# Windowed attention with a gated feed-forward block: the sigmoid gate made from tanh and exp instead of a reciprocal

## The chip, the cores and the metric

One Trainium2 chip, of which the kernel uses one core. The metric is the time of one launch on the device in microseconds (us). The core has five engines that run side by side and wait for one another by semaphores: TensorE (PE in the profile, with its weight loads shown apart as PEld), VectorE (DVE), ScalarE (ACT), GpSimd (POOL) and SyncE (SP), which issues the DMAs. Each engine works through its own instructions in order.

## The reference

The inputs are q, k, v of shape (8, 8, 576, 64) and the weights of a gated block, all float32. First comes attention in which each row sees itself and the 63 rows before it, then a block that mixes each row with the row before it:

```python
scores = scale * np.matmul(q, k.transpose(0, 1, 3, 2))
mask = (rel >= 0) & (rel < 64)                 # rel = row - column
attn = softmax(np.where(mask, scores, -1e9))   # with 1e-9 added to the sum
x = np.matmul(attn, v)                         # put together to (8, 576, 512)

x_prev = x shifted by one row
xk = mu_k * x + (1.0 - mu_k) * x_prev
xr = mu_r * x + (1.0 - mu_r) * x_prev
k = np.maximum(xk @ w_k, 0.0)                  # 512 -> 1024
v = k * k @ w_v                                # 1024 -> 512
r = 1.0 / (1.0 + np.exp(-(xr @ w_r)))          # the gate, 512 -> 512
return r * v
```

## The kernel before, in words

The rows of all batches lie one behind the other, 4608 in all, and are cut into blocks of 64. The gated block is computed in eleven *units* of 4, 5 and then nine times 7 blocks, so that a matmul of the units 2 to 10 has 448 columns. A unit has three phases on TensorE. The k phase makes `xk @ w_k` in 8 column tiles, the r phase `xr @ w_r` in 4, and the v phase `k*k @ w_v` in 4. Every float32 operand is split into a high and a low part, and a product takes three matmuls for each 128 rows of the contraction. So a k or r tile takes 12 matmuls and a v tile 24, and a unit 240. Unit 0 runs r, k, v, the others k, r, v.

The order is written out by hand: every engine keeps the order in which the Python code issues its work. Six matmuls of the gated block are one *step* of a clock, and a unit has 40 steps. Work is issued at a step (`at_step`) or so many steps later (`later(n, fn)`). Between the matmuls of the units stands the attention of later blocks, in *groups* of 8 blocks at the steps in the table `BEGIN`. A group goes like this:

- `scores`: 32 matmuls (`s<-k,q`).
- `soften`, for each half of the group: VectorE adds the mask and takes the row maximum, ScalarE takes exp and the row sum. Both write `pr`.
- `norm`: VectorE makes the reciprocal of the row sum (`rs`), GpSimd multiplies `pr` by it.
- `flip`: TensorE transposes `pr` (`t<-ident,pr`) into the one PSUM buffer `t`; `keep`: ScalarE copies that to SBUF (`COPY pt<-t`). The second half's flip stands two steps, 12 matmuls, behind the first's, and needs both its own normalized `pr` and the buffer `t` emptied by the first half's copy.
- `values`: matmuls with v (`x<-pt,v`), one group later, and a copy to `xT`.

The next unit's inputs are made by `mix`, in the steps 25 to 31 (xk) and 33 to 39 (xr) of a unit: VectorE makes `d` with two instructions for each piece, ScalarE rounds it to the high part (`CAST xk<-d`), GpSimd subtracts to get the low part (`xk<-d,xk`).

The change touches the end of an r tile (`r_units`) and the end of a v tile (`gated`). In the r phase, one step behind the last matmul of a tile ScalarE runs `power` on the tile's PSUM bank, and two steps behind it VectorE runs `share`. The result waits in one of four buffers `r` until the v tile of the same number is done. Then `gated` multiplies them on VectorE and SyncE stores the result. The pool tag `tmp` has five buffers that rotate among the weights' decoding (`wt`, at the start only), the mixed `d` and the k phase's `kf`.

At the start, to about 130 us, the weights arrive as float64 and are decoded to float32 by ScalarE and VectorE (`wt`, `wp`, `ws`), beside unit 0.

Of the kernel before, what the change touches and what calls it, by code (L numbers as in the profile page):

```python
# [9 lines left out]
F32 = mybir.dt.float32  # L10
F32R = mybir.dt.float32r
U32 = mybir.dt.uint32
AF = mybir.ActivationFunctionType
ALU = mybir.AluOpType
PSUM = bass.MemoryType.PSUM

P = 128
# [7 lines left out]
TU = max(UNITS) * W  # L25
# [3 lines left out]
FAR = 3.0e38  # L29
SCALE = 1.0 / D**0.5  # L30
R_BUFS = 4
WC = 512
XB = 9
TB = 5
# [15 lines left out]
def attn_rwkv_kernel(ctx, tc, qT, kT, v2, mu_k, mu_r, w_k, w_v, w_r, out):  # L50
# [5 lines left out]
    tmp = ctx.enter_context(tc.tile_pool(name="tmp", bufs=2))  # L56
# [16 lines left out]
    pe, dve, sca, pool = (Engine(e) for e in (nc.tensor, nc.vector, nc.scalar, nc.gpsimd))  # L73
# [3 lines left out]
    def later(steps, fn, *args):  # L77
        due.setdefault(now + steps, []).append((fn, args))
# [14 lines left out]
    for first in (None, 0, 1):  # L93
        masks[first] = const.tile([P, P], F32, name=f"mask{first}")
        nc.gpsimd.memset(masks[first], 0.0)
        for j in range(2):
            m = masks[first][j * W:(j + 1) * W]
# [218 lines left out]
    def parts(u):  # L316

        t, end = sum(UNITS[:u]) * W, sum(UNITS[:u + 1]) * W
        found = []
        while t < end:  # L320
            n = min(end, (t // S + 1) * S) - t
            found.append((t // S, t % S, n))
            t += n
        return found
# [22 lines left out]
    def weight(w, a, c, m):  # L347

        o = m * P
        return w[c, o // WC][:, a, o % WC:o % WC + P]  # L350

    def product(ps, w, col, x, n):

        for c in range(n):
            for a, e in ((0, 0), (0, 1), (1, 0)):
                pe.matmul(ps, weight(w, a, c, col), x(c, e), start=(c == 0 and a == e),
                          stop=(c == n - 1 and a == 1))
                yield

    def r_units(xr, gate, n):  # L360

        for m in range(NC):
            ps = ps_m.tile([P, 512], F32, name="m", tag="m")[:, :n]
            yield from product(ps, wr_s, m, lambda c, e: xr[:, e, c, :n], NC)

            def power(ps=ps):
                r = tmp.tile([P, TU], F32, name="r", bufs=R_BUFS)[:, :n]
                sca.activation(r, ps, AF.Exp, scale=-1.0)
                gate.append(r)

            def share(m=m):
                dve.tensor_scalar(gate[m], gate[m], FAR, 1.0, op0=ALU.min, op1=ALU.add)
                dve.reciprocal(gate[m], gate[m])

            later(1, power)
            later(2, share)

    def k_units(xk, k2, n):
# [21 lines left out]
                later(1 + i, fn)  # L400

    def gated(u, m, ps, o):
        dve.tensor_mul(o, ps, o)
        c0 = 0
        for b, t0, nt in parts(u):
            nc.sync.dma_start(out[b, m * P:(m + 1) * P, t0:t0 + nt], o[:, c0:c0 + nt])
            c0 += nt

    def v_units(u, k2, gate, n):
        for m in range(NC):  # L410
            ps = ps_m.tile([P, 512], F32, name="m", tag="m")[:, :n]
            yield from product(ps, wv_s, m, lambda c, e: k2[c][:, e], NF)
            later(1, gated, u, m, ps, gate[m])

    def v_first(u, k2, gate, n):


        acc = [ps_m.tile([P, 2, n], F32, name="mv", tag="m") for _ in range(NC // 2)]
        for f in range(NF):
            for m in range(NC):  # L420
                for a, e in ((0, 0), (0, 1), (1, 0)):
                    pe.matmul(acc[m // 2][:, m % 2], weight(wv_s, a, f, m), k2[f][:, e],
                              start=(f == 0 and a == e and m % 2 == 0),
                              stop=(f == NF - 1 and a == 1 and m % 2 == 1))
                    yield
        for m in range(NC):
            later(1, gated, u, m, acc[m // 2][:, m % 2], gate[m])
# [88 lines left out]
    for u, nb in enumerate(UNITS):  # L516
        n = nb * W
        xr, xk = mixed
        gate, k2 = [], []
# [12 lines left out]
        def work():  # L532
            if u == 0:
                yield from r_units(xr, gate, n)
                yield from k_units(xk, k2, n)
                yield from v_first(u, k2, gate, n)
            else:
                yield from k_units(xk, k2, n)
                yield from r_units(xr, gate, n)
                yield from v_units(u, k2, gate, n)  # L540
# [40 lines left out]
```

## Time and profile before

| | |
|---|---|
| median of 3 runs | 762.38 us (760.97 to 764.76) |
| the profiled execution | 762.73 us |
| its span, first to last instruction | 760.5 us |
| mean granted TensorE clock | 0.941 of full speed |
| busy: PE / DVE / ACT / POOL | 668.5 / 514.2 / 351.2 / 332.7 us |

The span leaves out 2.2 us of the profiled execution's own time. A line of the profile's groups names the engine, the operation, the tile written and those read (buffer numbers left out), and its shape; behind it stand the count, the busy time, the mean of one in ns, and the idle time of the engine before it with what ended that. Line L71 is the helper through which all compute instructions are issued, so tiles and not lines tell the instructions apart. `m` is a PSUM bank that a product is summed in, `ks` the split k*k, `ws` split weights. A timeline row gives the start, the duration, and in brackets how long the engine had stood idle and what it waited for.

### The profile page before, as it was taken

The page shows a single profiled execution, that of the slowest core. Times are in us where ns is not written, and L with a number is a line of the kernel's source. Part 1 is how long each engine was busy: PE and PEld are TensorE (multiplying, and loading weights), DVE is VectorE, ACT ScalarE, POOL GpSimd, SP SyncE. Part 2 cuts the span into 40 slices and gives each one's busy share as a digit, 9 for nine tenths or more (in the row PEclk, how much of TensorE's full clock was granted, in tenths as well). Part 3 has the DMA queues.
Part 4 walks back from the last instruction along what each step waited for, and adds up shares of the span by engine and source line. Part 5 has one row for each costly group of instructions (what it writes and reads, how often), then busy time and mean ns, then how long its engine had stood idle before and what let it go on. Part 6 is the DMA issues. An engine that isn't in the chain of part 4 may idle for free.

```text
span 760.5 us, 14297 instructions
## 1 busy us (share of the span) xinstructions
PE 668.5 (88%) x5232; PEld 593.7 (78%) x5232; DVE 514.2 (68%) x1328; ACT 351.2 (46%) x1067; POOL 332.7 (44%) x503
## 2 busy tenths in 40 slices
PE   3556657898998999899979989998998997999998
PEld 2446556887887888698869989887886996999997
DVE  4789797358439926954883595497388549739562
ACT  4556645544653455356434535534654562242330
POOL 4544645524651653445254355435425642432610
PEclk9958877999999899999999999999999999999999
DMA  7961201222310122132111112122221200100101
GB/s 243 302 245 63 84 32 60 87 72 92 109 60 28 69 72 77 59 127 84 60 38 60 38 60 85 59 72 97 64 84 56 84 1 7 43 0 13 37 1 49
DMA packets 33766, 56.50 MB, mean 74 GB/s; under 512 B 5024, under 2 KB 16800, under 8 KB 33696
## 3 DMA queue, kind: packets, MB, share of 16 engines
q1 hardware_dynamic: 33696, 55.59, 21.9%
q8 instruction: 41, 0.67, 0.4%
q14 instruction: 29, 0.24, 0.1%
HBM read 46.14 MB, written 9.44 MB: 73 GB/s over the span
## 4 chain that ended last, share of the span: by engine, by line
PE 52%; DVE 23%; issue 9%; ACT 7%; POOL 4%; DMA 3%; SPq 1%; POOLq 0%; ACTq 0%
PE m L71 41%; DVE r L71 9%; DVE d L71 6%; ACT pr L71 4%; PE s L71 4%; PE x L71 3%; PE t L71 3%; POOL pr L71 3%; DVE wp L71 2%; DVE pr L71 2%; DVE wt L71 2%; DMA w<-w_k 2%; DVE rs L71 2%; POOL kf L71 1%; PE mv L71 1%
## 5 line engine op out<-in xcount | busy, mean ns | idle before, releaser
L71 POOL TENSOR_SCALAR pr<-pr,rs 128x128 f32<-128x128 f32 x288 | 123.3, 447 | 232.3 <-DVE nmax L71 157.8
L71 PE MATMUL m<-xk,ws 128*128 128x448 f32 (+2 forms) x1056 | 215.8, 358 | 5.6 <-POOL ws L71 3.0
L71 PE MATMUL m<-ks,ws 128*128 128x448 f32 (+1 forms) x960 | 208.7, 375 | 0.0
L71 PEld LDWEIGHTS m<-xk,ws 128*128 128x128 f32 x1056 | 188.4, 191 | 18.5 <-POOL ws L71 3.2
L71 PEld LDWEIGHTS m<-ks,ws 128*128 128x128 f32 x960 | 184.0, 198 | 14.1
L71 ACT ACTIVATE pr<-pr,nmax 128x128 f32<-128x128 f32 x288 | 113.0, 395 | 79.9 <-DVE nmax L71 79.9
L71 DVE TENSOR_TENSOR ks<-kf,ks 128x448 fp32r<-128x448 f32 (+2 forms) x88 | 56.4, 640 | 125.3 <-ACT ks L71 125.3
L71 DVE RECIPROCAL r<-r 128x448 f32<-128x448 f32 (+2 forms) x44 | 121.9, 2771 | 1.5
L71 PE MATMUL t<-ident,pr 128*128 128x128 f32 x288 | 60.1, 315 | 65.7 <-ACT pt L71 42.6
L71 PE MATMUL m<-xr,ws 128*128 128x448 f32 (+2 forms) x528 | 112.6, 364 | 3.9 <-ACT xr L71 2.2
L71 POOL TENSOR_TENSOR kf<-kf 128x448 f32<-128x448 f32 (+2 forms) x88 | 78.0, 886 | 77.4 <-ACT kf L71 77.3
L71 PEld LDWEIGHTS t<-ident,pr 128*128 128x128 f32 x288 | 38.6, 153 | 86.3 <-POOL pr L71 44.4
L71 PEld LDWEIGHTS m<-xr,ws 128*128 128x128 f32 x528 | 95.5, 195 | 11.4 <-ACT xr L71 2.6
L71 ACT CAST ks<-kf 128x448 fp32r<-128x448 f32 (+2 forms) x88 | 47.5, 540 | 68.0 <-POOL kf L71 67.9
L71 DVE TENSOR_TENSOR d<-xT 128x256 f32<-128x256 f32 (+6 forms) x136 | 77.5, 570 | 0.1
L71 DVE CUSTOM_DVE_ANT_0 pr<-s,maskNone 128x128 f32<-128x128 f32 x224 | 55.0, 282 | 27.5 <-PE s L71 27.5
L71 POOL TENSOR_TENSOR xr<-d,xr 128x448 fp32r<-128x448 f32 (+2 forms) x44 | 51.5, 1176 | 35.3 <-ACT xr L71 35.0
L71 POOL TENSOR_TENSOR xk<-d,xk 128x448 fp32r<-128x448 f32 (+2 forms) x44 | 52.6, 1206 | 28.3 <-ACT xk L71 28.3
L71 ACT COPY xT<-x 128x256 f32<-128x256 f32 (+7 forms) x68 | 23.3, 391 | 70.6 <-PE x L71 70.6
L71 ACT ACTIVATION_READ_ACCUMULATOR pr<-pr,nmax 128x1 f32 x288 | 54.6, 190 | 0.0
L71 ACT COPY pt<-t 128x512 f32<-128x512 f32 (+1 forms) x74 | 42.2, 570 | 26.2 <-PE t L71 26.1
L71 PE MATMUL s<-k,q 64*64 64x128 f32 x1152 | 46.5, 305 | 6.6 <-DMA q<-qT 4.5
(42 smaller groups left out, 589.0 us busy)
## 6 DMA issues: line engine op xcount, KB each, us to landing
v<-v SPq DMA_DIRECT2D x56, 256.0 KB, 3.9
k<-kT SPq DMA_DIRECT2D x28, 288.0 KB, 2.8
q<-qT SPq DMA_DIRECT2D x28, 288.0 KB, 3.7
w<-w_k SPq DMA_DIRECT2D x8, 512.0 KB, 7.2
w<-w_v SPq DMA_DIRECT2D x8, 512.0 KB, 10.2
outT<-r SPq DMA_DIRECT2D x12, 224.0 KB, 1.9
w<-w_r SPq DMA_DIRECT2D x4, 512.0 KB, 4.9
outT<-r SPq DMA_DIRECT2D x12, 160.0 KB, 1.8
```

The costliest lines, as they stand in the source:

```text
L71: return lambda *args, **kw: tc.keep_in_program_order(op(*args, **kw))
```

## The change

The gate is computed in another way. For z = `xr @ w_r`, before: ScalarE makes exp(-z), VectorE clips it and adds 1, and takes the reciprocal. Now: ScalarE makes `th` = tanh(z/2) and `r` = exp(z). VectorE takes min(exp(z), 1), clears the sign bit of `th` by a bitwise and on its words read as integers, and makes (|th| + 1) * min(exp(z), 1), which is twice the gate. The factor 0.5 enters in `gated`, in the same instruction as the product with the v tile. `th` takes a buffer of the tag `tmp`.

```diff
         for m in range(NC):
             ps = ps_m.tile([P, 512], F32, name="m", tag="m")[:, :n]
             yield from product(ps, wr_s, m, lambda c, e: xr[:, e, c, :n], NC)
-
-            def power(ps=ps):
-                r = tmp.tile([P, TU], F32, name="r", bufs=R_BUFS)[:, :n]
-                sca.activation(r, ps, AF.Exp, scale=-1.0)
+            state = []
+
+            def powers(ps=ps, state=state):
+                state += [tmp.tile([P, TU], F32, name="th", tag="tmp", bufs=TB)[:, :n],
+                          tmp.tile([P, TU], F32, name="r", bufs=R_BUFS)[:, :n]]
+                sca.activation(state[0], ps, AF.Tanh, scale=0.5)
+                sca.activation(state[1], ps, AF.Exp)
+
+            def share(state=state):
+                th, r = state
+                dve.tensor_scalar(r, r, 1.0, None, op0=ALU.min)
+                dve.tensor_scalar(th.bitcast(U32), th.bitcast(U32), 0x7FFFFFFF, None, op0=ALU.bitwise_and)
+                dve.scalar_tensor_tensor(r, th, 1.0, r, op0=ALU.add, op1=ALU.mult)
                 gate.append(r)
 
-            def share(m=m):
-                dve.tensor_scalar(gate[m], gate[m], FAR, 1.0, op0=ALU.min, op1=ALU.add)
-                dve.reciprocal(gate[m], gate[m])
-
-            later(1, power)
+            later(1, powers)
             later(2, share)
...
     def gated(u, m, ps, o):
-        dve.tensor_mul(o, ps, o)
+        dve.scalar_tensor_tensor(o, ps, 0.5, o, op0=ALU.mult, op1=ALU.mult)
```

No instruction moves past another: on PE, POOL and SP the order is the same, and on VectorE and ScalarE the new ones stand where the old ones stood. Two places matter later. The first is VectorE in the r phase of unit 2, the first of 448 columns; `pr` and `nmax` belong to the group whose scores stand between the r tiles. Before:

```order
L71 TENSOR_SCALAR r<-r 128x448
L71 RECIPROCAL r<-r 128x448
L71 TENSOR_SCALAR r<-r 128x448
L71 RECIPROCAL r<-r 128x448
L71 TENSOR_SCALAR r<-r 128x448
L71 RECIPROCAL r<-r 128x448
L71 ISA pr,nmax<-s,mask_101 128x128
L71 ISA nmax 128x1
```

And now, in the same place:

```order
L71 TENSOR_SCALAR r<-r 128x448
L71 TENSOR_SCALAR th<-th 128x448
L71 SCALAR_TENSOR_TENSOR r<-th,r 128x448
L71 TENSOR_SCALAR r<-r 128x448
L71 TENSOR_SCALAR th<-th 128x448
L71 SCALAR_TENSOR_TENSOR r<-th,r 128x448
L71 TENSOR_SCALAR r<-r 128x448
L71 TENSOR_SCALAR th<-th 128x448
L71 SCALAR_TENSOR_TENSOR r<-th,r 128x448
L71 ISA pr,nmax<-s,mask_101 128x128
L71 ISA nmax 128x1
```

Two instructions for a tile have become three, and the next group's softmax still stands behind three r tiles.

The second place is ScalarE at the same time, from the end of the k phase to the fourth r tile; `pt` are the copies of the transposes, `xT` the attention's output. Before:

```order
L71 CAST ks<-kf 128x448
L71 ACTIVATE r<-m 128x448
L71 COPY pt<-t 128x512
L71 ACTIVATE r<-m 128x448
L71 COPY pt<-t 128x512
L71 ACTIVATE r<-m 128x448
L71 COPY xT<-x 128x512
```

And now:

```order
L71 CAST ks<-kf 128x448
L71 ACTIVATE th<-m 128x448
L71 ACTIVATE r<-m 128x448
L71 COPY pt<-t 128x512
L71 ACTIVATE th<-m 128x448
L71 ACTIVATE r<-m 128x448
L71 COPY pt<-t 128x512
L71 ACTIVATE th<-m 128x448
L71 ACTIVATE r<-m 128x448
L71 COPY xT<-x 128x512
```

Each copy of a transposed half now stands behind one activation more. The program has one row `ACT_TABLE_LOAD` on ScalarE, at its start, both before and now.

## The prediction

> **What bounds the kernel now.** I read the busy shares first, then the slices, then who waited for whom on TensorE, and last the time rows of the places where it waits.
>
> ```profile
> PE 668.5 (88%) x5232; PEld 593.7 (78%) x5232; DVE 514.2 (68%) x1328; ACT 351.2 (46%) x1067; POOL 332.7 (44%) x503
> PE   3556657898998999899979989998998997999998
> DVE  4789797358439926954883595497388549739562
> PE t L71 <- ACT pt L71: 42.6, 15, 5.3
> ```
>
> TensorE bounds the kernel, apart from the first 130 us. But it has regular dents, and VectorE is full (9) just where TensorE dents. Its longest waits stand in front of the transposes `t`. The dents lie in the r phases of units 1 to 8. Of their stretches, here are unit 2's, ten us within it, unit 8's, and the time after that:
>
> ```profile
> core 0: us, PE busy (x) PEld busy (x) DVE busy (x) ACT busy (x) POOL busy (x), PEclk, DMA share, GB/s
> 220.00:256.00 36.00, 32.95 (x250) 27.48 (x250) 30.68 (x71) 14.95 (x46) 13.65 (x22) 0.91 0.14 47
> 230.00:240.00 10.00, 10.00 (x103) 8.77 (x102) 9.88 (x16) 2.90 (x12) 0.00 (x0) 1.00 0.17 54
> 620.00:652.00 32.00, 26.97 (x177) 23.22 (x176) 26.61 (x45) 10.98 (x31) 10.70 (x14) 0.89 0.02 8
> 650.00:760.00 110.00, 106.85 (x546) 99.57 (x544) 64.88 (x76) 29.57 (x54) 32.63 (x29) 1.00 0.07 24
> ```
>
> TensorE idles 3.1 us in unit 2's row and 5.0 in unit 8's, and its mean clock is 0.91 and 0.89. In the last row no attention is left, and it runs without a dent. Unit 2 shows the mechanism:
>
> ```profile
> 227.69 0.54 ACT L71 ACTIVATE r<-m 128x448 f32<-128x448 f32 x1
> 228.13 0.58 ACT L71 COPY pt<-t 128x512 f32<-128x512 f32 x1
> 228.85 0.63 PE L71 MATMUL t<-ident,pr 128*128 128x128 f32 x4
> 231.87 1.10 PE L71 MATMUL s<-k,q 64*64 64x128 f32 x32
> 235.25 2.95 DVE L71 RECIPROCAL r<-r 128x448 f32<-128x448 f32 x1
> 238.39 0.41 ACT L71 ACTIVATE pr<-pr,nmax 128x128 f32<-128x128 f32 x1 [3.70 <-DVE nmax L71]
> 241.52 1.48 PE L71 MATMUL t<-ident,pr 128*128 128x128 f32 x4
> 241.72 2.95 DVE L71 RECIPROCAL r<-r 128x448 f32<-128x448 f32 x1
> 246.64 0.56 ACT L71 CAST xk<-d 128x448 fp32r<-128x448 f32 x1 [0.91 <-DVE d L71]
> 247.07 2.27 POOL L71 TENSOR_SCALAR pr<-pr,rs 128x128 f32<-128x128 f32 x4 [3.35 <-DVE rs L71]
> 247.84 1.25 PE L71 MATMUL t<-ident,pr 128*128 128x128 f32 x3 [2.44 <-ACT pt L71]
> 249.40 0.47 PE L71 MATMUL t<-ident,pr 128*128 128x128 f32 x1 [0.31 <-POOL pr L71]
> 254.26 1.10 PE L71 MATMUL s<-k,q 64*64 64x128 f32 x32
> ```
>
> The scores are done at 233, but VectorE is in the third of three reciprocals until 238.2, and the group's softmax stands behind them. The fourth reciprocal (241.7 to 244.7) holds up its second half. Where the wait is called `ACT pt`, the copy stands on ScalarE behind a `CAST xk` that itself waits for VectorE's `d`: here too VectorE is late.
>
> **What the dents cost.** From the first of these two flips to the next scores there are 8 transposes and 24 matmuls. Undisturbed, the same takes 5.84 us:
>
> ```profile
> 409.61 0.60 PE L71 MATMUL t<-ident,pr 128*128 128x128 f32 x4
> 415.45 1.10 PE L71 MATMUL s<-k,q 64*64 64x128 f32 x32
> 570.87 1.51 PE L71 MATMUL t<-ident,pr 128*128 128x128 f32 x4 [0.87 <-POOL pr L71]
> 582.05 1.10 PE L71 MATMUL s<-k,q 64*64 64x128 f32 x32
> 249.87 4.46 PE m L71 x12
> 413.11 2.41 PE m L71 x12
> ```
>
> In unit 2 it took 254.26 - 241.52 = 12.74, an excess of 6.9 us. That holds the idle time, transposes that go at GpSimd's pace, and 12 matmuls at a lower clock afterwards (4.46 for 2.41, in the last two rows, which are of the chain). Unit 7, in the middle rows, has 582.05 - 570.00 - 5.84 = 6.2, with its first flip wanted 0.87 before it starts. The same difference in units 3 to 6 gives 6.5, 6.9, 2.3 and 5.0. Unit 8, with half the transposes and no scores behind, has some 7.5, and unit 1, whose matmuls have 320 columns, 6.0. Together 47 us (6.0+6.9+6.5+6.9+2.3+5.0+6.2+7.5 = 47.3).
>
> On the clock, the Trainium skill's page "TensorE: Matmul & The Clock Gate" (section "HAM oscillation — how this bites in real kernels") says that idle gaps above about 3.4 us let the clock fall. By that rule unit 2's wait of 2.44 us would have cost no speed, and only units with longer gaps would lose any; some 8 us of the loss (the slow matmuls of the five units with shorter gaps, 1 to 2 us each) would then have another cause and might stay, for a time near 723. The trace differs: the clock mean is 0.91 over unit 2's row and the 12 matmuls took 4.46 us, so I count the slow matmuls with the gap that they follow.
>
> **The change part by part.**
>
> ```profile
> L71 DVE RECIPROCAL r<-r 128x448 f32<-128x448 f32 x36 | 106.3, 2953 | 1.2
> L71 DVE TENSOR_SCALAR r<-r 128x448 f32<-128x448 f32 x36 | 13.5, 376 | 1.5 <-ACT r L71 1.5
> L71 DVE TENSOR_TENSOR ks<-kf,ks 128x448 fp32r<-128x448 f32 x72 | 45.2, 627 | 114.2 <-ACT ks L71 114.2
> L71 DVE SCALAR_TENSOR_TENSOR d<-d,mur,xT 128x448 f32<-128x448 f32 x12 | 11.3, 941 | 0.4
> L71 DVE TENSOR_SCALAR wp<-wt 128x512 uint32<-128x512 uint32 x20 | 13.9, 695 | 0.7
> L71 ACT ACTIVATE r<-m 128x448 f32<-128x448 f32 x36 | 19.5, 541 | 14.6 <-PE m L71 14.6
> L71 ACT ACT_TABLE_LOAD x1 | 1.3, 1283 | 0.7 <-PEq L573 0.7
> ```
>
> VectorE, a tile of 448: out goes the reciprocal, 2.95 us. The clip stays one TENSOR_SCALAR of 0.38. The bitwise and is not in the trace; it lies between the float form, 0.38, and the integer form into PSUM, 0.69. I take 0.38, since it reads and writes SBUF as that does. The new (|th|+1)*min lies between two-tensor rows, 0.63 and 0.94; I take 0.64, as it has no operand by partition. So 3.33 becomes 1.40, a saving of 1.9 us (1.3 at the dear ends), and 7.7 for a unit's four (5.3). That is 70 us of VectorE's busy time on 36 tiles, of which only what lay in the dents counts.
>
> Does that clear a dent? Unit 2's first half-softmax, at 238.1, stood behind three tiles. They now end near 234: scores at 233, third exp at about 232, 1.4 behind it. The four behind it make the second half 6 to 7.5 us earlier. TensorE wants that half at 241.52 + 0.35 + 2.5 = 244.4 and had finished its transposes at 249.9 for 244.8, so 5 are needed: the dent goes, with 1 to 2 us to spare. The late link next is ScalarE's `COPY pt` behind `CAST xk`, which moves forward with `d`. Units 4 and 8 have the least to spare; in unit 8 I leave 0.5. With the dear ends, 5.3 just covers 5, and some 1 us would remain in each unit. In unit 1 the first pair of flips has a wait that isn't this one:
>
> ```profile
> 164.88 0.43 ACT L71 ACTIVATE r<-m 128x320 f32<-128x320 f32 x1
> 165.21 0.58 ACT L71 COPY pt<-t 128x512 f32<-128x512 f32 x1
> 165.93 0.63 PE L71 MATMUL t<-ident,pr 128*128 128x128 f32 x4 [1.87 <-ACT pt L71]
> ```
>
> It is outside the 47 and stays.
>
> ScalarE: 44 Tanh more, each as an exp of the same shape, 541 ns and in a row 0.44 from start to start (227.69 to 228.13). That is 23 us on an engine that is 46% busy. On the path it counts where a `COPY pt` stands behind the first r tile and a flip waits for it: 0.33 in unit 1 and 0.44 in units 2, 3 and 4, together 1.7 us lost. In units 5 to 8 that copy ends well ahead of its flip. `th` in `tmp`: five buffers back lies a `kf` of two or more tiles before, long read, so I cost it at nothing; were it not, ScalarE would wait ahead of the same copies. The PSUM bank is freed 0.5 later, and three more rotate: nothing. The product with 0.5 is one two-input instruction for another, nothing; on the last tile it could show 0.1 either way.
>
> Unit 0: its first two tiles stand on the chain that feeds the decoded weights; this is the first.
>
> ```profile
> 49.96 1.75 DVE r L71
> ```
>
> At 256 columns I estimate 0.7 for the two new instructions, from 1.02 at 448, so twice 1.05 are saved there; beyond 60 us the chain runs over ScalarE, where a Tanh adds to it. I take 2, with bounds of 0 and 4.2 (four tiles). Units 9 and 10 have no attention beside them, and TensorE doesn't wait there: nothing.
>
> Sum, against the profiled 762.73 (its span 760.5 and 2.2 around it; the median of the runs is 0.35 lower): 762.7 - 47.3 + 0.5 + 1.7 - 2.0 = 715.6, and a little stays somewhere, so 716. The best is all of it with 4.2 in unit 0 and no loss to Tanh: 711, or 709 with the first pairs also earlier. With the dear ends, 8 us stay: 724.
>
> **The rivals.** *Half the relief.* GpSimd and VectorE disturb each other: an instruction on `d` seems to take longer while GpSimd subtracts (the mean of 941 for `d`'s second instruction against 627 for two tensors speaks for it). If the earlier VectorE work meets more of that, or `COPY pt` stays late behind `CAST xk`, a unit keeps 1 us of idle and 1.6 of slow matmuls: 8 times 2.5 is 20 us, giving 736. Against it: VectorE has 5 us idle in unit 2's 36, and with 7.7 less work will have more.
>
> *Slower, by tables.* If Tanh and Exp did not lie in one activation table, each r tile would cost two loads of 1.283. In a unit that is 4 x 2.57 + 4 x 0.44 = 12 us on ScalarE ahead of the copies and of the softmax's exps, against 7.7 saved on VectorE. It decides from 1.9 us of ScalarE for a tile. The net 4.3 in 8 units gives 762.7 + 34 = 797. Against it: the changed program has one row of a load, as before. The Trainium skill's page "ScalarE: Activation LUTs" (section "Table sets: the hidden batching unit") lists exp and tanh in one set and asks for one load; the program's row agrees, and no run here shows Tanh yet.
>
> *Slower, by contention.* The three short instructions might be stretched by GpSimd, as the row below was at most (least, median and greatest ns): to 0.9, 1.57 and 1.57, say, 4.0 for 3.3 us. Then each dent grows by up to 2.7 and a Tanh: 762.7 + 8 x 3.1 = 788. It decides from 1.9 us of stretch in a tile. Against it: GpSimd does nothing in the row 230 to 240 of unit 2.
>
> ```profile
> L71 DVE TENSOR_SCALAR wt<-wt x20: 363/446/1567, 9.5 to 121.9; 128x512 f32<-128x512 f32 x20
> ```
>
> *Hidden anyway.* The dents are ScalarE's own, as unit 1's first one, and the time stays at 760 to 764. The nmax wait of 3.70 in unit 2 speaks against it.
>
> **Chances.** Dents gone (709 to 727): 0.75. Half the relief (727 to 755): 0.17. No change (within 0.5%, 3.8 us, about what a measurement here can tell): 0.03. Tables: 0.01. Contention: 0.04. So faster 0.92, same 0.03, slower 0.05. The range is 709 to 736: it holds the first case and about half of the second.
>
> **What the profile would show.** Right: VectorE's busy time near 440 us, ScalarE's near 375, no wait over 1 us in front of `t` in units 2 to 8, a clock of 1.00 there, and TensorE busy in nines from 190 us on. Unit 1's first wait is still there, at 2.2. Wrong: the new two-tensor form far above 0.64, more than one table load, or waits of `t` for `ACT pt` that VectorE's `d` no longer explains.

## The result, and the profile after

The changed kernel takes 718.85 us (median of 4 runs, 718.43 to 719.55) against 761.82 us (760.97 to 764.76) for the kernel before on the same chip: a ratio of 0.943, with a 95% interval of 0.9403 to 0.9458. Some 43 us are gone. The profiled execution took 719.05 us, 716.8 of it span, at a mean clock of 0.957 (before 0.941).

First the busy times and the slices of the page after, then the row of the waits on TensorE in front of `t` for `pt` (us in total, times, the longest):

```profile
PE 650.5 (91%) x5232; PEld 584.0 (81%) x5232; DVE 444.1 (62%) x1372; ACT 367.2 (51%) x1111; POOL 339.0 (47%) x503
PE   4547665988999999999999999999999999999997
DVE  4888887537636944873693584487368548638241
```

```profile
PE t L71 <- ACT pt L71: 26.3, 14, 4.5
```

TensorE's row of digits has lost its regular eights: from the eleventh slice on it is nines, except the last. In those slices VectorE has two nines where it had seven. VectorE lost 70.1 us of busy time, ScalarE gained 16.0. The waits for `pt` fell from 42.6 to 26.3, with 14 waits and the longest of 4.5 in the start. Two stretches by engine, over the r and v phases of unit 2 and of unit 8 (mean clock behind the busy times):

```profile
core 0: us, PE busy (x) PEld busy (x) DVE busy (x) ACT busy (x) POOL busy (x), PEclk, DMA share, GB/s
215.00:251.00 36.00, 35.48 (x290) 32.05 (x289) 29.10 (x95) 21.09 (x69) 17.56 (x28) 1.00 0.19 62
585.00:620.00 35.00, 34.85 (x228) 31.23 (x227) 27.76 (x63) 13.84 (x35) 14.03 (x17) 1.00 0.06 21
```

TensorE idles 0.5 and 0.15 us where it idled 3.1 and 5.0, and the clock is whole. Unit 2 again, by time rows:

```profile
222.52 0.54 ACT L71 ACTIVATE th<-m 128x448 f32<-128x448 f32 x1
222.96 0.54 ACT L71 ACTIVATE r<-m 128x448 f32<-128x448 f32 x1
223.38 0.59 ACT L71 COPY pt<-t 128x512 f32<-128x512 f32 x1
224.11 0.63 PE L71 MATMUL t<-ident,pr 128*128 128x128 f32 x4 [0.52 <-ACT pt L71]
227.08 1.10 PE L71 MATMUL s<-k,q 64*64 64x128 f32 x32
233.06 0.62 DVE L71 SCALAR_TENSOR_TENSOR r<-th,r 128x448 f32<-128x448 f32 x1
236.51 0.60 PE L71 MATMUL t<-ident,pr 128*128 128x128 f32 x4
237.02 2.27 POOL L71 TENSOR_SCALAR pr<-pr,rs 128x128 f32<-128x128 f32 x4 [1.60 <-PE t L71]
239.42 0.60 PE L71 MATMUL t<-ident,pr 128*128 128x128 f32 x4
242.35 1.10 PE L71 MATMUL s<-k,q 64*64 64x128 f32 x32
```

From the first flip to the next scores it is 242.35 - 236.51 = 5.84 us, the undisturbed time, where before it was 12.74. But the margin is thin: GpSimd's last `pr` ends at 239.29 (237.02 + 2.27) and the second flip starts at 239.42. And the first pair of flips (224.11) has a wait of 0.52 that it did not have, behind the Tanh at 222.52.

What VectorE and ScalarE pay for a tile, from the groups of instructions (count, then busy time and mean ns of one), and below them the spread of the new product (least, median and greatest ns):

```profile
L71 DVE TENSOR_SCALAR r<-r 128x448 f32<-128x448 f32 x36 | 14.2, 395 | 17.2 <-ACT r L71 16.7
L71 DVE TENSOR_SCALAR th<-th 128x448 uint32<-128x448 uint32 x36 | 14.0, 388 | 0.0
L71 DVE SCALAR_TENSOR_TENSOR r<-th,r 128x448 f32<-128x448 f32 x36 | 22.6, 627 | 1.3
L71 ACT ACTIVATE th<-m 128x448 f32<-128x448 f32 x36 | 19.6, 545 | 12.3 <-PE m L71 12.3
L71 ACT ACT_TABLE_LOAD x1 | 1.3, 1283 | 0.7 <-PEq L578 0.7
```

```profile
L71 DVE SCALAR_TENSOR_TENSOR r<-th,r x44: 424/625/671, 48.9 to 695.8; 128x448 f32<-128x448 f32 x36, 128x256 f32<-128x256 f32 x4, 128x320 f32<-128x320 f32 x4
```

A tile is 0.395 + 0.388 + 0.627 = 1.41 us on VectorE instead of 3.33.

Where the 43.6 us of span came from can be read from one place for each group of scores: its first matmul's start before, minus after. In unit 2 that difference is 231.87 - 227.08 = 4.79 at one group and 254.26 - 242.35 = 11.91 at the next, so 7.1 were won between them, in the dent. The same subtraction along the trace gives the table. Two units need another mark. In unit 1 the scores between the two pairs of flips themselves ran at two speeds, so its rows go from the first pair's first flip (161.71 - 158.50 = 3.2) to the second pair's (175.77 - 174.37 = 1.4) and on to the scores behind (186.42 - 181.35 = 5.1). Unit 8 has no scores behind its dent, so its row goes on to the end of the span.

| place | predicted | measured |
|---|---|---|
| unit 0 | 2.0 | 1.6 |
| dent of unit 1 | 6.0 | 3.7 |
| dents of units 2, 3, 4 | 6.9, 6.5, 6.9 | 7.1, 6.7, 6.7 |
| dents of units 5, 6, 7 | 2.3, 5.0, 6.2 | 2.3, 5.0, 6.2 |
| dent of unit 8 | 7.5 - 0.5 | 7.2 |
| first pair of flips, unit 1 | -0.33 | -1.8 |
| first pairs, units 2, 3, 4 | -0.44 each | -0.36 each |
| a new wait at the end of unit 7 | 0 | -1.4 |

Another 1.6 was won in unit 1's k phase, ahead of its r tiles, and the small remainders of the other groups all but cancel. As far as the traces show, those 1.6 are luck: a flip waits 1.87 us there before and 1.84 in after, and only before were the 12 matmuls and the scores behind it slow (2.69 and 1.99 us, against 2.00 and 1.10). In the run below with the new form in units 0, 9 and 10 alone, where unit 1 is as before, they were not slow either (2.01 behind 1.84).

### The profile page after: what moved, and what is told of

It reads as the page before. It is cut to its first block, busy times and chain, and to the rows that moved or that the text cites. A ratio compares the mean times of both kernels' runs of the same rounds, so it can differ in the third digit from the quotient of the medians.

```text
span 716.8 us, 14398 instructions
## 1 busy us (share of the span) xinstructions
PE 650.5 (91%) x5232; PEld 584.0 (81%) x5232; DVE 444.1 (62%) x1372; ACT 367.2 (51%) x1111; POOL 339.0 (47%) x503
## 4 chain that ended last, share of the span: by engine, by line
PE 74%; DVE 12%; ACT 6%; DMA 4%; issue 2%; SPq 1%; POOL 1%; ACTq 0%; POOLq 0%
PE m L71 59%; PE s L71 5%; PE x L71 4%; PE t L71 4%; DVE d L71 4%; DVE wp L71 3%; DVE wt L71 2%; ACT pr L71 2%; DMA v<-v 2%; DMA w<-w_v 1%; ACT wt L71 1%; DVE pr L71 1%; POOL pr L71 1%; PE mv L71 1%; DVE r L71 1%
## 5 line engine op out<-in xcount | busy, mean ns | idle before, releaser
L71 POOL TENSOR_SCALAR pr<-pr,rs 128x128 f32<-128x128 f32 x288 | 127.7, 461 | 189.1 <-DVE nmax L71 147.7
L71 PE MATMUL m<-ks,ws 128*128 128x448 f32 (+1 forms) x960 | 197.0, 361 | 0.0
L71 PEld LDWEIGHTS m<-ks,ws 128*128 128x128 f32 x960 | 174.4, 188 | 12.0
L71 PE MATMUL m<-xr,ws 128*128 128x448 f32 (+2 forms) x528 | 114.5, 368 | 3.7 <-ACT xr L71 1.9
L71 PEld LDWEIGHTS m<-xr,ws 128*128 128x128 f32 x528 | 97.0, 198 | 11.4 <-POOL xr L71 2.7
L71 PE MATMUL t<-ident,pr 128*128 128x128 f32 x288 | 54.3, 302 | 41.4 <-ACT pt L71 26.3
L71 POOL TENSOR_TENSOR xk<-d,xk 128x448 fp32r<-128x448 f32 (+2 forms) x44 | 54.8, 1255 | 23.6 <-ACT xk L71 23.6
L71 DVE SCALAR_TENSOR_TENSOR d<-d,mur,xT 128x256 f32<-128x256 f32 (+6 forms) x68 | 49.1, 722 | 2.4
```

Of the source, the lines that this page charges most:

```text
L71: return lambda *args, **kw: tc.keep_in_program_order(op(*args, **kw))
```

## The experiments

The experiments ran in two series, on two chips, and each ratio is to the kernel before in its own series. That kernel took 763.03 us (median of 19 runs, 760.99 to 767.71) in the first series, which holds the next four experiments, and 763.13 us (9 runs, 761.91 to 766.2) in the second, which holds the rest.

### The Tanh alone, the reciprocal kept

```diff
-                sca.activation(state[1], ps, AF.Exp)
+                sca.activation(state[1], ps, AF.Exp, scale=-1.0)
...
-                dve.tensor_scalar(r, r, 1.0, None, op0=ALU.min)
-                dve.tensor_scalar(th.bitcast(U32), th.bitcast(U32), 0x7FFFFFFF, None, op0=ALU.bitwise_and)
-                dve.scalar_tensor_tensor(r, th, 1.0, r, op0=ALU.add, op1=ALU.mult)
+                dve.tensor_scalar(r, r, FAR, 1.0, op0=ALU.min, op1=ALU.add)
+                dve.reciprocal(r, r)
...
-        dve.scalar_tensor_tensor(o, ps, 0.5, o, op0=ALU.mult, op1=ALU.mult)
+        dve.tensor_mul(o, ps, o)
```

> The kernel before with the Tanh alone added: ScalarE has both activations, VectorE clips and takes the reciprocal as before, the Tanh's result is not used. Theory A (the gain is VectorE's: the group's softmax stands in VectorE's order behind the r tiles, and a tile became 1.9 us shorter): no gain, and the Tanh's own price on the first pair of flips of units 1 to 4, 1 to 4 us, so 763 to 766 where the kernel before has 762. Theory B (part of the gain lies on ScalarE, by the changed times at which it frees PSUM banks and copies the transposes): 755 or less.

Measured: 763.52 us (10 runs, 761.47 to 767.54), ratio 0.9985 (0.9959 to 1.0012). TensorE's digits keep the dents of before, and the first pair of flips in unit 2 shows the price of the Tanh:

```profile
PE   3656567988998999899979989998998996999997
```

```profile
229.69 0.63 PE L71 MATMUL t<-ident,pr 128*128 128x128 f32 x4 [0.53 <-ACT pt L71]
```

So the gain is not the Tanh's, nor that of any change in ScalarE's order. The price of the Tanh (0.38 to 0.43 at each of three first pairs, by the group starts) is smaller than the spread of these runs.

### The new VectorE form without the Tanh

The second activation is left out: `th` is `r`, and both sides of the product read the exp.

```diff
-                state += [tmp.tile([P, TU], F32, name="th", tag="tmp", bufs=TB)[:, :n],
-                          tmp.tile([P, TU], F32, name="r", bufs=R_BUFS)[:, :n]]
-                sca.activation(state[0], ps, AF.Tanh, scale=0.5)
-                sca.activation(state[1], ps, AF.Exp)
+                state.append(tmp.tile([P, TU], F32, name="r", bufs=R_BUFS)[:, :n])
+                sca.activation(state[0], ps, AF.Exp)
...
-                th, r = state
+                th = r = state[0]
```

> The changed kernel without the Tanh, which is left out of the computation: VectorE still has its three short instructions, now all on the exp's tile; ScalarE has one activation for a tile. Theory A: the waits of 0.52 us in the r phases of units 2, 3 and 4 and a part of unit 1's 2.17 go, so 1.5 to 3.5 us less than the changed kernel's 718.9: 715 to 717.5. Theory B: the time does not move by more than 0.5, or it gets longer.

Measured: 718.98 us (4 runs, 717.03 to 719.32), ratio 0.9406 (0.937 to 0.9442): no faster than the change, a miss for theory A. The trace shows why. At the first pairs of units 2, 3 and 4 it does win 0.4 each, and at unit 1's 1.8. But in unit 1 some 1.7 of that is given back behind the second pair, and 0.9 more was lost in the start, which differs between executions. Unit 1's flips in this kernel, and the 12 matmuls behind the last of them:

```profile
163.60 0.63 PE L71 MATMUL t<-ident,pr 128*128 128x128 f32 x4 [1.86 <-ACT pt L71]
176.28 0.71 PE L71 MATMUL t<-ident,pr 128*128 128x128 f32 x2 [0.50 <-ACT pt L71]
177.82 0.33 PE L71 MATMUL t<-ident,pr 128*128 128x128 f32 x1 [0.84 <-POOL pr L71]
178.71 3.32 PE L71 MATMUL m<-ks,ws 128*128 128x320 f32 x12
```

The wait for the copy is 0.50 us where it was 0.26 in after, so only 0.2 of the loss is waiting for VectorE and GpSimd. The rest is the slow matmuls, 3.32 us instead of 2.00, and the scores behind them. They can't be put down to the missing Tanh: in the second series the changed kernel itself had the waits of after in front of this pair (0.26, 0.84 and 0.47) and 3.33 us behind it.

### The new form on half of each unit's tiles

Tiles 0 and 1 of each unit take the new form, tiles 2 and 3 the old.

```diff
+    def new_form(u, m):
+        return m < 2
...
-            later(1, powers)
-            later(2, share)
+            later(1, powers if new_form(u, m) else power_old)
+            later(2, share if new_form(u, m) else share_old)
```

`power_old` and `share_old` are those of the kernel before, and `gated` multiplies such a tile as before.

> The new form in the first two r tiles of every unit, the reciprocal in the last two. Theory A: a dent ends when VectorE is about 5 us earlier; two tiles give 3.9, so the second flips still wait 1 to 2 us in most units, unit 5 and 6 not at all, unit 8 longer: 725 to 734. Rival P (every us of VectorE saved is worth the same, half the tiles half the gain): 740.

Measured: 735.05 us (4 runs, 734.15 to 738.19), ratio 0.9628 (0.958 to 0.9677), 1 us above the range of theory A and below rival P, whose 740 lies outside the interval: half of VectorE's saving (478.9 us busy) gives some 65% of the gain (0.0372 of 0.057 by the ratios). By unit it is not a share at all. Dents 2 to 7 give back 5.7, 5.0, 4.9, 2.3, 4.2 and 4.2 of their 7.1, 6.7, 6.7, 2.3, 5.0 and 6.2; unit 8 gives 1.4 of 7.2. In unit 8 the old tiles stand just ahead of the half-softmax:

```profile
606.52 2.95 DVE L71 RECIPROCAL r<-r 128x448 f32<-128x448 f32 x1
609.93 0.40 ACT L71 ACTIVATE pr<-pr,nmax 128x128 f32<-128x128 f32 x1 [3.87 <-DVE nmax L71]
617.36 0.36 ACT L71 COPY pt<-t 128x256 f32<-128x256 f32 x1
617.87 0.66 PE L71 MATMUL t<-ident,pr 128*128 128x128 f32 x2 [3.46 <-POOL xk L71]
```

The exps of the softmax wait 3.87 us for `nmax`, which VectorE makes behind that reciprocal. The second flip's wait of 3.46 is put down to GpSimd by the profile, but it also needs `t` emptied, and that copy ends only at 617.72. A dent is set by how much VectorE work stands ahead of a given softmax, not by the engine's total.

### The new form where no dent lies

The same switch with another condition.

```diff
+    def new_form(u, m):
+        return u in (0, 9, 10)
```

> The new form in units 0, 9 and 10 alone, the reciprocal in units 1 to 8: 12 of 44 tiles. Theory A: in units 9 and 10 no softmax stands behind the r tiles, so only unit 0's 1.6 us are gained: 759.5 to 761.5 where the kernel before has 762. Rival P (gain in proportion to VectorE's time saved): some 10 us, 752.

Measured: 761.5 us (10 runs, 759.55 to 765.64), ratio 0.9976 (0.9951 to 1.0), although VectorE's busy time fell by 20 us:

```profile
PE 671.9 (88%) x5232; PEld 593.0 (78%) x5232; DVE 494.5 (65%) x1340; ACT 355.4 (47%) x1079; POOL 332.1 (44%) x503
```

That is 1.5 us by the medians, and the interval ends at 0.49%, 3.7 us, well short of rival P's 10. Unit 0 is worth 1.2 us by the group starts. That nothing is won behind unit 8 is read from the ends of the chains of work, first of before and then of after, whose units 9 and 10 differ in the gate:

```profile
651.04 105.82 PE m L71 x528
```

```profile
607.39 105.82 PE m L71 x528
```

528 matmuls take 105.82 us in both; the tail only begins earlier. This run's own trace can't be used for it. Its profiled execution was the slowest of the ten (765.64), and its tail took 3.5 us longer, with TensorE as busy and the clock at 1.00 to 700 us and 0.99 behind, as before:

```profile
650.48 109.31 PE m L71 x528
```

What slowed it is open.

### The changed kernel again, and the activations one step later

In the second series the changed kernel ran once more, unaltered.

> The changed kernel again, beside the next three on one chip: 718 to 720.

Measured: 721.17 us (5 runs, 718.11 to 722.76), ratio 0.9435 (0.9405 to 0.9465), above the range expected, with the same ratio as in the result. The profiled execution is the slowest of the five and 3.7 us longer in span than the one above: 1.7 of that builds up over five groups of units 5 and 6 in steps of 0.3 to 0.4, with TensorE busy throughout and the clock at 1.00. Why is open.

Then the activations and the VectorE step were put one step later, so that the copy of the first pair runs ahead of the Tanh:

```diff
-            later(1, powers)
-            later(2, share)
+            later(2, powers)
+            later(3, share)
```

> The changed kernel with the r tile's activations and VectorE instructions issued one step later, so that the copy of the transposes stands ahead of the Tanh on ScalarE. Theory A: the first pairs' waits of 0.52 us in units 2, 3 and 4 go (they cost 0.36 each); in unit 1 what is won at the first pair is lost at the second, as without the Tanh; a second flip may be late where there is little to spare (units 4 and 7): 717 to 719. Rival: a step's delay (1.2 us) of the r tiles on VectorE uses up the 1 to 2 us to spare in each unit, 720 to 724.

Measured: 728.7 us (5 runs, 727.33 to 729.83), ratio 0.9545 (0.9518 to 0.9572): 7.5 us slower than the change in the same series, worse than both theories. The first pairs won 0.7 each in units 2, 3 and 4, as meant. But part of the dents came back, 1.2 to 1.7 us each in units 2, 3, 4 and 7, and unit 0 lost 3.3. In unit 1 the 2.2 won at the first pair went again at the second, with 1.4 more. Unit 2 in this kernel:

```profile
238.86 1.20 POOL L71 TENSOR_TENSOR xk<-d,xk 128x448 fp32r<-128x448 f32 x1 [0.89 <-ACT xk L71]
239.09 1.45 DVE L71 SCALAR_TENSOR_TENSOR r<-th,r 128x448 f32<-128x448 f32 x1
240.57 0.60 PE L71 MATMUL t<-ident,pr 128*128 128x128 f32 x4
242.58 2.27 POOL L71 TENSOR_SCALAR pr<-pr,rs 128x128 f32<-128x128 f32 x4 [2.53 <-DVE rs L71]
247.58 1.10 PE L71 MATMUL s<-k,q 64*64 64x128 f32 x32
```

The fourth tile's product now falls between the halves of the softmax and beside GpSimd's subtraction, where it takes 1.45 us instead of 0.62. GpSimd's `pr` waits for `rs` and starts 2.0 us after the flip's start instead of 0.5, and from flip to scores it is 7.01 us, 1.2 over the undisturbed 5.84. A shift of one step, some 1.2 us, uses up the whole margin.

### A gate with Tanh alone

ScalarE's Tanh is the only step on the r tile: sigmoid(z) = (1 + tanh(z/2))/2, with the 1 added in the product and the 0.5 taken into the scale of the Relu that is squared.

```diff
-                state += [tmp.tile([P, TU], F32, name="th", tag="tmp", bufs=TB)[:, :n],
-                          tmp.tile([P, TU], F32, name="r", bufs=R_BUFS)[:, :n]]
+                state.append(tmp.tile([P, TU], F32, name="r", bufs=R_BUFS)[:, :n])
...
-                sca.activation(state[1], ps, AF.Exp)
-
-            def share(state=state):
-                th, r = state
-                dve.tensor_scalar(r, r, 1.0, None, op0=ALU.min)
-                dve.tensor_scalar(th.bitcast(U32), th.bitcast(U32), 0x7FFFFFFF, None, op0=ALU.bitwise_and)
-                dve.scalar_tensor_tensor(r, th, 1.0, r, op0=ALU.add, op1=ALU.mult)
-                gate.append(r)
+                gate.append(state[0])
...
-            later(2, share)
...
-                sca.activation(state[0], ps, AF.Relu)
+                sca.activation(state[0], ps, AF.Relu, scale=0.5**0.5)
...
-        dve.scalar_tensor_tensor(o, ps, 0.5, o, op0=ALU.mult, op1=ALU.mult)
+        dve.scalar_tensor_tensor(o, o, 1.0, ps, op0=ALU.add, op1=ALU.mult)
```

> The gate as (1 + tanh(z/2)) in the output's product alone, with the factor 0.5 put into the k phase's relu (scaled by the root of 0.5): no exp, and no VectorE instruction at the r tile. VectorE does 1.4 us less for a tile, ScalarE 0.44 less. Theory A (TensorE bounds after the change): only what is left of waits can go, the first pairs' 0.36 in units 2 to 4, 1.4 in unit 7, 0.4 in unit 4 and 1 to 2 in unit 1: 714 to 717. Rival P (VectorE's time counts in proportion): 70 us of VectorE saved gave 43, so 60 more give 37: 682.

Measured: 713.16 us (4 runs, 712.23 to 713.74), ratio 0.9337 (0.9313 to 0.9362), 0.8 below theory A's range and far from rival P's 682.

```profile
PE 648.0 (91%) x5232; PEld 583.8 (82%) x5232; DVE 384.6 (54%) x1240; ACT 349.7 (49%) x1067; POOL 335.1 (47%) x503
```

VectorE is rid of another 60 us, where the change took 70 from it, and the time falls by 8.0 us against the changed kernel in the same series (5.7 against the 718.85 of the result). By the group starts, against the trace of after, 2.5 lies in unit 1, most of it because no slow matmuls follow its first pair, and 0.43 at each first pair of units 2, 3 and 4, since the second activation is gone there. Once the dents are closed, VectorE's time is no longer what ends last.

The same with its activation one step later (`later(2, powers)` in place of `later(1, powers)`):

> The last kernel with its one activation a step later, behind the copy of the transposes. Theory A: 0.1 to 0.3 less in units 2 to 4 and some in unit 1, so the last one's time less 0 to 1.5: 713 to 716.

Measured: 712.43 us (4 runs, 711.79 to 713.38), ratio 0.933 (0.9305 to 0.9355), 0.6 below theory A's range. It is not to be told from the former: the medians are 0.7 apart and the runs overlap. In the trace the first pairs won 0.7 instead of 0.43, and no dent came back, as here no VectorE step hangs on the activation. The Tanh-only gate, in either order, beats both kernels.

## Why the prediction was right

716 us were predicted, in a range of 709 to 736, and 718.85 came out. The case foreseen as the likeliest, all dents gone, is what happened.

**The dents.** The sum of 46.8 for the eight dents (47.3 less 0.5) became 44.9 in the table. Seven of the eight terms are within 0.3 us, unit 8's with the 0.5 allowed to it. The half-tile run shows the mechanism, the run with units 0, 9 and 10 shows that the gain is not elsewhere, and the Tanh beside the reciprocal shows that it is VectorE's. Of the rivals, tables and contention did not come: one `ACT_TABLE_LOAD`, and no product above 671 ns. With the activations one step later, though, a product did take 1.45 us beside GpSimd, so such a stretch does exist in another order. One reading of place was wrong: the waits of the dents do not lie in the r phases, but 36 to 66 matmuls into the v phases (the matmuls behind them are `m<-ks,ws`); what belongs to the r phases is the VectorE work that makes them late.

**Unit 1 was mis-sized.** Its dent gave 3.7 and not 6.0. What held the rest is no reciprocal (rows of after, 172 to 180 us):

```profile
174.30 1.45 DVE L71 SCALAR_TENSOR_TENSOR d<-d,muk,xT 128x448 f32<-128x448 f32 x1
176.22 3.06 POOL L71 TENSOR_SCALAR pr<-pr,rs 128x128 f32<-128x128 f32 x4 [0.95 <-DVE rs L71]
178.53 0.33 PE L71 MATMUL t<-ident,pr 128*128 128x128 f32 x1 [0.84 <-POOL pr L71]
```

GpSimd's four products take 3.06 us beside VectorE's work on `d`, 0.8 more than in unit 2, and the last transposes go at its pace. The step that failed was to take the whole excess over an undisturbed unit as VectorE's lateness; a part of it was GpSimd's rate, which stays. The gate with Tanh alone gives the size. There VectorE does nothing at an r tile, and from flip to scores unit 1 still takes 179.13 - 172.80 = 6.33 us, with 3.06 for the four products, where after takes 6.98 and the prediction's undisturbed time is 10.65 - 6.0 = 4.65. So of the 2.3 that stayed, 0.65 hung on VectorE's r tiles and 1.7 did not. The "half the relief" rival had this mechanism, but it cost time in this one unit only; in unit 2 it took from the margin.

**The Tanh ahead of the copies.** 0.44 each in units 2, 3 and 4 became 0.36. In unit 1 the wait grew from 1.87 to 2.17, as expected (0.33), and then 12 matmuls of 320 columns took 3.1 us instead of 2.0:

```profile
163.03 0.63 PE L71 MATMUL t<-ident,pr 128*128 128x128 f32 x4 [2.17 <-ACT pt L71]
163.41 3.12 PE L71 MATMUL m<-xr,ws 128*128 128x320 f32 x12
```

The scores behind them were slow too (1.51 for 1.10), so the term was 1.8. I had priced a longer wait by its length alone, and had counted slow matmuls only behind the waits that go. But this is one execution: in the second series' execution of the same kernel the wait was 2.19, the 12 matmuls took 2.01, and the term was the 0.3 that was priced. There the slow matmuls stood behind unit 1's second pair instead. From the first pair to the end of unit 1 the change gains 1.9 us in both executions, where 5.7 (6.0 - 0.33) was predicted.

**A wait that was not foreseen.** At the end of unit 7 the second flip of a pair now waits 1.37, for a copy behind a `CAST xr` behind VectorE's `d`:

```profile
556.81 0.56 ACT L71 CAST xr<-d 128x448 fp32r<-128x448 f32 x1 [2.13 <-DVE d L71]
557.28 0.58 ACT L71 COPY pt<-t 128x512 f32<-128x512 f32 x1
558.01 0.63 PE L71 MATMUL t<-ident,pr 128*128 128x128 f32 x4 [1.37 <-ACT pt L71]
```

The late link named in the prediction, a copy behind a cast, is the one that shows here, in another phase. These three terms (2.3 + 1.5 + 1.4 = 5.2) and the 0.4 that unit 0 gave less, less the 1.6 won by luck in unit 1's k phase and 0.6 of small gains in the other rows, account for the 3.4 us by which the sum of 715.6 lay under the profiled 719.05. So the number is nearer than the terms in unit 1.

**The margin.** "1 to 2 us to spare" in a unit was wrong, and nothing in the time showed it: after's rows leave 0.13 us in unit 2, and the activations one step later brought part of the dents back. The profile says that GpSimd's `pr` waited for the first flip there, but `rs` came from VectorE just as late:

```profile
236.67 0.18 DVE L71 RECIPROCAL rs<-rs 128x4 f32<-128x4 f32 x1
```

It ends at 236.85 and `pr` starts 0.17 later, the same distance as before (246.90 to 247.07), where the wait is called `rs`. Counted from the group's scores `pr` started 15.20 us behind them before and 9.94 in after, so it came 5.3 us earlier, and not 6 to 7.5; some 0.8 of that went to one instruction on `d` beside GpSimd (the last section). The step at fault counted from VectorE's tiles to the half-softmax, and not on through `d`, `rs` and GpSimd's `pr` to the flip.

**The clock.** The Trainium skill's page "TensorE: Matmul & The Clock Gate" (section "HAM oscillation — how this bites in real kernels") puts the loss of speed at idle gaps above about 3.4 us, and by that the slow matmuls behind shorter gaps would have had another cause and could have stayed. The trace decides otherwise: in units 2 to 8 they went with the gaps. In unit 2 the flip-to-scores time is the undisturbed one, and the stretch's clock is 1.00.

**The signs.** VectorE's busy time is 444.1 us (near 440 predicted) and ScalarE's 367.2 (375). Unit 1's first wait is 2.17 (2.2). One sign did not hold: in units 2 to 8 there is a wait above 1 us for `t`, the 1.37 at the end of unit 7.

## What to carry to other kernels

Price a shorter instruction by the work that stands ahead of a particular late result in its engine's order, not by the engine's busy time: 70 us off VectorE gave 43 where the dents were, 20 us off it beside no dent gave 1 to 2, within the noise, and another 60 gave 6 to 8. A dent costs more than its idle time, since the matmuls behind it can be slow, so a wait that grows from 1.9 to 2.2 can cost several times its growth, as it did in one of two executions. When a stall has gone, follow the chain on to the consumer to learn what is left of margin, and prefer the form with the fewest steps: a shift of one place undid a sixth of the gain here.

## What the runs showed of the hardware

**Slow matmuls can follow waits of 2 us and more.** Of before, two places: the 12 matmuls of 448 columns behind unit 2's wait of 2.44, and a wait of 2.06 in front of `t` in unit 5 with the 12 behind it.

```profile
249.52 4.80 PE L71 MATMUL m<-ks,ws 128*128 128x448 f32 x12
...
452.47 0.63 PE L71 MATMUL t<-ident,pr 128*128 128x128 f32 x4 [2.06 <-ACT pt L71]
452.86 2.70 PE L71 MATMUL m<-ks,ws 128*128 128x448 f32 x12
```

After 2.44 us they took 4.80, after 2.06 they took 2.70, against 2.65 to 2.71 where nothing was waited for. In the traces of all these kernels, from 130 us on, single waits of 1 to 2.15 us cost nothing with 448 columns, 2.39 to 2.46 always 1 to 2.2 us, and 2.71 two times out of three. With 320 columns, where 12 take 2.0 us, 1.84 to 1.87 mostly cost nothing (twice 0.7 to 1.0), and 2.17 to 2.19 cost 1.1 to 1.4 in half the cases. At unit 1's second pair, where three waits follow one another, even 0.26, 0.84 and 0.47 were once followed by 3.33 us and once by 2.00.

**An instruction of VectorE can wait out one of GpSimd.** In unit 2 of after:

```profile
234.24 1.18 POOL L71 TENSOR_TENSOR xk<-d,xk 128x448 fp32r<-128x448 f32 x1
234.45 1.12 DVE L71 SCALAR_TENSOR_TENSOR d<-d,muk,xT 128x128 f32<-128x128 f32 x1
237.59 0.35 DVE L71 SCALAR_TENSOR_TENSOR d<-d,muk,xT 128x128 f32<-128x128 f32 x1
```

The second instruction of the same shape as the third takes 1.12 us instead of 0.35, and ends 0.15 after GpSimd's (235.57 against 235.42). The Trainium skill's page "SBUF — State Buffer" (section "SBUF: two separate sides") says that the two engines share a pair of ports, and that whichever starts first, a GpSimd instruction or one of VectorE with two inputs in SBUF, keeps it for the whole instruction. Both inputs here, `d` and `xT`, lie in SBUF, and these rows agree, as does the 1.45 of the activations one step later, which ends 0.48 after the GpSimd instruction that began 0.23 ahead of it.

**The reciprocal is dear by the element.** 2953 ns for 448 columns and 1752 for 256 (before) make (2953 - 1752) / 192 = 6.3 ns for a column, while the integer and on `th`, 388 ns for 448, costs as little as the float form beside it, 395.
